# Routing attention and bilinear FFN on one core: row sums of the first batch element moved to VectorE, weight checks moved to ScalarE

## The chip, the cores and the metric

The kernel runs on one core of a Trainium2 chip. The time is the device time of one execution in microseconds (us), as the median of repeated runs. A profile of one execution shows what each engine did: TensorE (PE: matmuls, and PEld: its weight loads), VectorE (DVE), ScalarE (ACT), GpSimd (POOL) and SyncE (SP), whose queue issues most transfers. All five work through their own instructions in order and wait for each other by semaphores.

## What is computed

Attention with a mask by clusters, then a feed-forward block (FFN) with a product of two linear maps. There are 4 batch elements, 8 heads, 768 positions and 64 values per head; the FFN goes from 512 to 1536 and back, on 3072 tokens.

```python
q_assign = argmax(einsum('bhsd,hcd->bhsc', q_n, c_n))      # the nearest of 16 centroids
k_assign = argmax(einsum('bhsd,hcd->bhsc', k_n, c_n))
mask   = q_assign[:, :, :, None] == k_assign[:, :, None, :]
scores = where(mask, scale * q @ k^T, -1e9)
attn   = exp(scores - max) / (sum + 1e-9)
x      = (attn @ v) as (4*768, 512)
out    = ((x @ w_a) * (x @ w_b)) @ w_out
```

The weights come as float64, read as 64-bit integers. The kernel makes float32 of them itself.

## The kernel before

Two heads form a pair; there are 16 pairs, 4 to a batch element (`HP` = 4). A pair has 12 units: 2 halves of the query positions (`hf`), each with 6 tiles of 128 key positions (`j`). The main loop goes through groups of 2 units, so 6 groups to a pair and 24 (`BG`) to a batch element; `l` is the place of the group in its pair. In group g TensorE computes the scores of the two units of g, and weighs `v` with the probabilities of the group before. The FFN of a batch element, cut into pieces, is strewn over later groups.

```python
def score(us):          # TensorE: one-hot masks times masks plus q times k; ScalarE: exp
    ...
    add(ohTs, True); add(qkTs, False); exp()

def add_up(u):          # sums of the probabilities over the key tiles of a half
    p, hf, j = where(u)
    if j == 0 or j == NJ - 1 and p < HP:
        return
    ...
    for a in range(2):
        many = p >= HP and (a == 1 or j in (2, 4))
        eng = nc.gpsimd if many else nc.vector
        eng.tensor_tensor(out=acc[:, a, :], in0=..., in1=probs[u][:, a, :], op=ALU.add)

def denominators(p, hf):   # ones times sums, on TensorE; for p < HP the last tile is added here
    terms = [acc]
    if p < HP:
        terms.insert(0, probs[p * UPP + hf * NJ + NJ - 1])
    for n, t in enumerate(terms):
        for a in range(2):
            nc.tensor.matmul(out=ps[a * D:(a + 1) * D, 0:HB], lhsT=ones, rhs=t[:, a, :], ...)
    nc.scalar.activation(out=den, in_=ps[:, 0:HB], func=AF.Copy, accum_out=stat[:, n:n + 1])

def normalize(p, hf):   # transpose, reciprocal, transpose on VectorE, then x times it on GpSimd
    return [across, invert, back, apply]
```

Each part of the weights (36 of 128x512) is loaded into one of two `raw` buffers, turned into float32 by four VectorE operations and a sum on GpSimd, and set to zero where the source is too small (below `SMALLEST` in the upper 32 bits, read as a float):

```python
def round_w(i):
    flush_w()
    ...                                            # four VectorE operations on raw
    nc.scalar.activation(out=size, in_=halves(FP32)[:, :, 1], func=AF.Abs)
    nc.gpsimd.tensor_tensor(out=w, in0=w, in1=rest, op=ALU.add)
    flush.append((w, size))

def flush_w():                                     # w = w * (size >= SMALLEST), on VectorE
    ...
```

For the pairs of the first batch element (p < HP) q and k are transposed by TensorE. From pair 4 on (`by_blocks`), VectorE transposes them, finds the nearest centroids, makes the one-hot masks and transposes those; eight transfers on SyncE's queue then put them into `ohT`, which the scores of the pair's first group read:

```python
def one_hot():
    nc.gpsimd.tensor_tensor(out=oh[KT], ..., op=ALU.subtract)
    v.tensor_tensor(out=oh[QT], ..., op=ALU.is_equal)
def one_hot_across():
    v.transpose(out=ohT, in_=oh...)
    for a in range(2):
        for kq in range(4):
            nc.sync.dma_start(out=ohTs[p][...], in_=ohT[r:r + NC, :])
```

The main loop, in the order in which the instructions are queued:

```python
due = {3 * i + 1: [i] for i in range(8)}           # the group in which a part is rounded
for i in range(8, len(w_parts)):
    due.setdefault(23 + int((i - 8) / 1.5), []).append(i)
...
for g in range(NG + 3):
    p, l = divmod(g, GPP)
    if 0 < g < NG: score(now)
    check_inverses()
    if 0 < g <= NG:
        for u in before: add_up(u)
    flush_w()
    if 0 < g <= NG: weigh(before)
    if g < NG: ready[l]()                          # steps that prepare the next pair
    late = int(g > EARLY)                          # EARLY = BG + 1
    if g % 3 == late and 0 < g - late:
        denominators(*divmod(g // 3 - 1, 2))
    round_next()                                   # round_w(i), then load_w(i + 2)
    first, second = (4, 1) if g <= EARLY else (5, 3 if g < NG else 2)
    ...                                            # normalize the half that is due
    ...                                            # pieces of the FFN, as far as the credit goes
    round_next()
    while todo: todo.popleft()()                   # what ready and normalize left to do
    ...                                            # transposes and loads of coming pairs
```

Ahead of the loop the masks of pair 0 are made, and TensorE fills its gaps there with idle transposes (`keep_busy`).

Of the kernel before, what the change touches and what calls it, by code (L numbers as in the profile page):

```python
# [26 lines left out]
SIGN_EXP = 0xFF800000 - 2 ** 32  # L27

SMALLEST = 1.125 * 2.0 ** -15

P = 128
SCALE = 0.125
# [3 lines left out]
def kernel(  # L36
# [94 lines left out]
                          skip_runtime_bounds_check_because="a count of rows")  # L131
    with tc.If(redo > 0):
        with ExitStack() as slow:
            long_path(nc, tc, slow, c, q, k, v, out)


def short_path(nc, tc, ctx, c, cn, centroids_in, casts, n_far, q, k, v,
# [51 lines left out]
    def load(p):  # L189
        if p >= NPAIR:  # L190
            return
        b, hp = divmod(p, HP)
        if by_blocks(p):
            t = qkp.tile([P, 2, S // 32, 32], FP32, name="qk")
            for w, src in enumerate((q, k)):
                for n in range(4):
                    a, d = divmod(n, 2)
                    nc.sync.dma_start(
                        out=t[32 * n:32 * n + 32, w],
                        in_=src[b, 2 * hp + a, :, 32 * d:32 * d + 32].rearrange(  # L200
                            "(j t) d -> t j d", t=32))
            qks[p] = t
            return
        t = qkp.tile([P, 2, NJ, 2, D], FP32, name="qk")
        for w, src in enumerate((q, k)):
            for a in range(2):
                nc.sync.dma_start(
                    out=t[:, w, :, a, :],
                    in_=src[b, 2 * hp + a].rearrange("(p j) d -> p j d", j=NJ))
        qks[p] = t  # L210
# [30 lines left out]
            in_=v[b, 2 * hp:2 * hp + 2].rearrange("a (p j) d -> p a (j d)", j=NJ))  # L241

    first = load_first()
    centroids_in()
    order_first(*first, 0, nc.vector.tensor_copy)
    order_first(*first, 1, nc.scalar.copy)
# [14 lines left out]
        nc.sync.dma_start(out=raw, in_=w_parts[i][1])  # L261
        raws[i] = raw

    flush = []

    def round_w(i):
        flush_w()
        w = w_parts[i][0]
        wi = w.bitcast(INT32)
        raw = raws.pop(i)  # L270
        halves = lambda dt: raw.bitcast(dt).rearrange("p (n two) -> p n two", two=2)
        lo, hi = halves(UINT32)[:, :, 0], halves(INT32)[:, :, 1]


        nc.vector.tensor_scalar(out=wi, in0=hi, scalar1=3, scalar2=0x3FFFFFF8,
                                op0=ALU.logical_shift_left,
                                op1=ALU.bitwise_and)
        nc.vector.scalar_tensor_tensor(out=wi, in0=hi, scalar=SIGN_TOP, in1=wi,
                                       op0=ALU.bitwise_and, op1=ALU.bitwise_or)

        rest = wtp.tile([P, WN], FP32, name="rest")
        nc.vector.tensor_scalar(out=rest.bitcast(INT32), in0=wi,
                                scalar1=SIGN_EXP, scalar2=None,
                                op0=ALU.bitwise_and)
        nc.vector.scalar_tensor_tensor(out=rest, in0=lo, scalar=2.0 ** -52,
                                       in1=rest, op0=ALU.mult, op1=ALU.mult)

        size = sizep.tile([P, WN], FP32, name="size")
        nc.scalar.activation(out=size, in_=halves(FP32)[:, :, 1], func=AF.Abs)
        nc.gpsimd.tensor_tensor(out=w, in0=w, in1=rest, op=ALU.add)  # L290
        flush.append((w, size))

    def flush_w():

        while flush:
            w, size = flush.pop(0)
            nc.vector.scalar_tensor_tensor(out=w, in0=size, scalar=SMALLEST,
                                           in1=w, op0=ALU.is_ge, op1=ALU.mult)

    stat = zero.tile([P, 4 * NPAIR], FP32, name="stat")  # L300
    nfar = zero.tile([P, 1], FP32, name="nfar")
    nc.vector.memset(nfar, -FAR)

# [32 lines left out]
    def prep_transpose(p, i):  # L336
        if i == 0:
            qkTs[p] = qtp.tile([P, 2 * S], FP32, name="qkT")
        ps = ps_m.tile([P, 512], FP32, name="m")
        for n in range(4):  # L340
            w, j = divmod(4 * i + n, NJ)
            nc.tensor.transpose(  # L342
                out=ps[:, n * P:(n + 1) * P],
                in_=qks[p][:, w, j].rearrange("p a d -> p (a d)"),
                identity=ident)
        dst = qkTs[p][:, i * 512:(i + 1) * 512]
        if p == 0 and i != 1:
            nc.vector.tensor_copy(out=dst, in_=ps)
        else:
            nc.scalar.copy(out=dst, in_=ps)  # L350
# [146 lines left out]
    def prep_steps(p):  # L497
        if p >= NPAIR:
            return [lambda: None] * 6

        def both(*fs):
            return lambda: [f() for f in fs]

        if by_blocks(p):
            steps = prep_by_blocks(p)
            ready = [lambda s=s: todo.extend(s) for s in steps]
            ready[1] = both(lambda: prep_sim(p), lambda: load_v(p), ready[1])
            return ready

        return [  # L510
            both(lambda: prep_transpose(p, 0), lambda: prep_transpose(p, 1)),
            both(lambda: prep_sim(p), lambda: load_v(p)),
            lambda: todo.extend(prep_assign(prep_across(p))),
            lambda: None,
            lambda: prep_onehot(p, 1),
            lambda: None,
        ]
# [40 lines left out]

    def add_up(u):
        p, hf, j = where(u)  # L560
        if j == 0 or j == NJ - 1 and p < HP:
            return
        if j == 1:
            accs[p, hf] = accp.tile([P, 2, HB], FP32, name="acc")
        acc = accs[p, hf]
# [3 lines that stand above are left out]
            eng.tensor_tensor(  # L569
                out=acc[:, a, :],  # L570
                in0=probs[u - 1][:, a, :] if j == 1 else acc[:, a, :],
                in1=probs[u][:, a, :], op=ALU.add)
# [19 lines left out]

    def denominators(p, hf):


        ps = ps_m.tile([P, 512], FP32, name="m")
        acc = accs.pop((p, hf))
        terms = [acc]
        if p < HP:
            terms.insert(0, probs[p * UPP + hf * NJ + NJ - 1])  # L600
        for n, t in enumerate(terms):
            for a in range(2):
                nc.tensor.matmul(out=ps[a * D:(a + 1) * D, 0:HB], lhsT=ones,  # L603
                                 rhs=t[:, a, :], start=(n == 0),
                                 stop=(n == len(terms) - 1))
        den = acc[:, 0, :]
        n = 4 * p + 2 * hf
        nc.scalar.activation(out=den, in_=ps[:, 0:HB], func=AF.Copy,
                             accum_out=stat[:, n:n + 1])
        den_of[p, hf] = acc  # L610
# [367 lines left out]
    def ffn_ready(p, hf):  # L978
# [28 lines left out]
    PER_GROUP = [int(cols / n) + 1 for cols, n in (  # L1007
        (UP + DOWN * 7 / 8, BG + 5.8), ((UP + DOWN) * 7 / 8, BG + 0.8),
        ((UP + DOWN) * 7 / 8, BG + 0.5))]
    EARLY = BG + 1  # L1010
    credit = 0

# [1 line left out]
    for i in range(8, len(w_parts)):  # L1016
        due.setdefault(23 + int((i - 8) / 1.5), []).append(i)

    keep_busy(18)
    prep_transpose(0, 0)  # L1020
    centroids_across()
    prep_transpose(0, 1)
# [2 lines left out]
    for r, factor in ((slice(0, P // 2), 1.0), (slice(P // 2, P), FAR)):  # L1025
        nc.vector.tensor_scalar(out=rank_far[r], in0=rank[r], scalar1=factor,
                                scalar2=None, op0=ALU.mult)
    load(1)
    load_v(0)
    load_w(0)  # L1030
    load_w(1)
# [3 lines left out]

    across = prep_across(0)
    rest_of_first = score((0, 1))
    keep_busy(4)
    for kq in range(2):
        for step in prep_assign(across, kq):  # L1040
            step()
        prep_onehot_first(kq)
        if kq == 0:
            keep_busy(5)
            rest_of_first()
            keep_busy(7)
    for g in range(NG + 3):
        p, l = divmod(g, GPP)
        if l == 0:
            ready = prep_steps(p + 1)  # L1050
        now = (2 * g, 2 * g + 1)
        before = (2 * g - 2, 2 * g - 1)
        if 0 < g < NG:
            score(now)
        check_inverses()
        if 0 < g <= NG:
            for u in before:
                add_up(u)
        flush_w()
        if 0 < g <= NG:  # L1060
            weigh(before)
        if g < NG:
            ready[l]()
        late = int(g > EARLY)
        if g % 3 == late and 0 < g - late:
            denominators(*divmod(g // 3 - 1, 2))
        parts = due.get(g, [])

        def round_next():
            if parts:  # L1070
                i = parts.pop(0)
                round_w(i)
                load_w(i + 2)

        round_next()
        if g <= EARLY:
            first, second = 4, 1
        else:
            first, second = 5, 3 if g < NG else 2
        ph = {first: (p, 0), second: (p - 1, 1)}.get(l)  # L1080
        halved = ph in den_of
        if halved:
# [16 lines left out]
        if halved:  # L1099
            ffn_ready(*ph)  # L1100
        if l == 0 and p + 1 < NPAIR:
            if not by_blocks(p + 1):
                prep_transpose(p + 1, 2)
            load(p + 2)
        if l == 4 and p + 1 < NPAIR and not by_blocks(p + 1):
# [7 lines left out]

    some_ffn(6)
    check_inverses()
    fine = zero.tile([P, 4 * NPAIR], FP32, name="fine")
    nc.vector.tensor_scalar(out=fine, in0=stat, scalar1=LIMIT, scalar2=None,
                            op0=ALU.is_le)
    least = zero.tile([P, 1], FP32, name="least")
# [9 lines left out]
    some_ffn(len(ffn))  # L1129


def long_path(nc, tc, ctx, c, q, k, v, out):

    B, H, S, D = q.shape
    NC = 16
# [15 lines left out]
    ps_o = pool("l_ps_o", 1, PS)  # L1151
    ident, rank, cT = c["ident"], c["rank"], c["cT"]
    R = 2 * NC


    far = lone.tile([R, 2], FP32, name="far")
# [198 lines left out]
```

## Time and profile before

| what | value |
|---|---|
| time, median of 3 runs | 1052.72 us (1052.52 to 1053.35) |
| span of the profile | 1050.6 us |
| PE busy | 1036.5 us, 99% |
| DVE busy | 709.6 us, 68% |
| POOL busy | 355.7 us, 34% |
| ACT busy | 260.6 us, 25% |
| granted TensorE clock, mean | 0.999 |

The first part of the page gives the busy time of every engine. Matmuls overlap in the records, so the busy time of PE is not a sum of the single durations, and the mean of one matmul is longer than the distance to the next. The chain of waits follows the work that ended last back to its beginning: each piece has a start, a length, an engine and a line of the kernel. A timeline lists the instructions of a stretch in order of time, with the idle time ahead of one in brackets. Instruction names are given as output<-inputs.

### The profile page before, as it was taken

The numbers are of one execution on the slowest core, as the hardware profiler recorded it, in microseconds if no ns is written. First come the engines' busy times: TensorE is split into PE (matmuls) and PEld (weight loads), VectorE is DVE, ScalarE is ACT, GpSimd is POOL, SyncE is SP. The second block draws the span as 40 slices with busy tenths as digits, with TensorE's granted clock in tenths as the row PEclk, the third lists the DMA queues.
The fourth block names the chain that finished last, engine by engine and source line by source line (L and its number), as shares of the span: only waits on it lengthen the run. The fifth ranks groups of instructions, "written<-read, shape, count | busy, mean of one in ns | idle before, by whom it ended". The sixth has DMA issues, their size and how long they took to land.

```text
span 1050.6 us, 17937 instructions
## 1 busy us (share of the span) xinstructions
PE 1036.5 (99%) x7156; PEld 510.6 (49%) x7156; DVE 709.6 (68%) x1402; ACT 260.6 (25%) x501; POOL 355.7 (34%) x329
## 2 busy tenths in 40 slices
PE   8999999999999999999999999999999999999997
PEld 5444444444445554444444555444444565444576
DVE  5778878787857548676767746767665846776752
ACT  5666333333322221212222121122121200000000
POOL 1111244555542323443545422444344310212200
PEclk9999999999999999999999999999999999999999
DMA  5334243526230130303020030300000000000001
GB/s 167 89 75 109 69 122 88 126 81 143 64 50 16 33 53 18 44 4 46 4 46 1 25 66 20 51 1 20 1 4 1 12 31 22 1 1 1 2 32 34
DMA packets 120523, 46.49 MB, mean 44 GB/s; under 512 B 106608, under 2 KB 115824, under 8 KB 120432
## 3 DMA queue, kind: packets, MB, share of 16 engines
q1 hardware_dynamic: 120016, 44.85, 18.4%
q8 instruction: 58, 0.95, 0.4%
q10 hardware_dynamic: 416, 0.43, 0.1%
q14 instruction: 33, 0.27, 0.1%
HBM read 37.78 MB, written 6.29 MB: 42 GB/s over the span
## 4 chain that ended last, share of the span: by engine, by line
PE 92%; DVE 5%; issue 1%; POOL 1%; ACT 0%; DMA 0%; DVEq 0%; POOLq 0%
PE m L654 61%; PE s L539 14%; PE O L580 12%; PE m L603 2%; PE m L358 1%; DVE raw L730 1%; PE m L342 1%; POOL xT L635 1%; DVE raw L757 0%; DVE xT L730 0%; DVE raw L874 0%; DVE ha L784 0%; DVE acc L630 0%; DVE acc L569 0%; DVE acc L623 0%
## 5 line engine op out<-in xcount | busy, mean ns | idle before, releaser
L548 ACT ACTIVATE pt<-s 128x768 f32<-128x768 f32 x192 | 145.4, 808 | 303.3 <-PE s L539 250.3
L569 POOL TENSOR_TENSOR acc<-acc,pt 128x384 f32<-128x384 f32 x144 | 152.8, 1076 | 57.9 <-ACT pt L548 41.9
L789 POOL TENSOR_TENSOR h<-h,ha 128x384 f32<-128x384 f32 x72 | 73.0, 1021 | 230.9 <-DVE ha L784 230.9
L580 PE MATMUL O<-pt,v 128*64 128x384 f32 x768 | 145.0, 499 | 0.0
L539 PE MATMUL s<-qkT 64*128 64x384 f32 x768 | 139.6, 483 | 0.0
L654 PE MATMUL m<-xT,wa_sb 128*64 128x384 f32 x672 | 119.3, 487 | 1.7 <-POOL xT L635 0.9
L654 PE MATMUL m<-xT,wb_sb 128*64 128x384 f32 x672 | 119.1, 486 | 0.0
L784 DVE TENSOR_TENSOR ha<-ha,m 128x384 f32<-128x384 f32 x126 | 66.9, 546 | 70.7 <-PE m L654 69.6
L784 DVE TENSOR_TENSOR h<-h,m 128x384 f32<-128x384 f32 x126 | 67.2, 548 | 61.1 <-PE m L654 60.4
L569 DVE TENSOR_TENSOR acc<-acc,pt 128x384 f32<-128x384 f32 x96 | 73.7, 793 | 36.0 <-POOL acc L569 35.1
L580 PEld LDWEIGHTS O<-pt,v 128*64 128x64 f32 x768 | 46.6, 136 | 86.2 <-issue 86.1
L654 PE MATMUL m<-wo_sb,h 128*64 128x256 f32 x768 | 86.7, 379 | 0.0
L539 PEld LDWEIGHTS s<-qkT 64*128 64x128 f32 x768 | 70.5, 187 | 31.4 <-issue 0.2
L635 POOL TENSOR_TENSOR xT<-xT,acc 128x384 f32<-128x384 f32 x32 | 33.0, 1033 | 143.4 <-DVE acc L630 143.4
L654 PEld LDWEIGHTS m<-xT,wa_sb 128*64 128x64 f32 x672 | 49.2, 137 | 61.3 <-issue 50.6
L654 PEld LDWEIGHTS m<-xT,wb_sb 128*64 128x64 f32 x672 | 49.2, 137 | 59.3 <-issue 55.4
L654 PE MATMUL m<-raw 128*64 128x384 f32 x384 | 70.2, 486 | 1.1 <-DVE ha L784 1.1
L654 PEld LDWEIGHTS m<-wo_sb,h 128*64 128x64 f32 x768 | 57.3, 137 | 28.3 <-issue 3.9
L654 PE MATMUL m<-xT,h 128*64 128x256 f32 x576 | 64.8, 379 | 0.1
L654 PEld LDWEIGHTS m<-xT,h 128*64 128x64 f32 x576 | 43.0, 137 | 20.9 <-issue 2.9
L654 PE MATMUL m<-xT,size 128*64 128x384 f32 x288 | 52.6, 486 | 0.0
L539 PE MATMUL s<-ohT 64*128 64x384 bf16 x384 | 48.1, 328 | 0.5 <-DVE ohT L441 0.5
(160 smaller groups left out, 1267.8 us busy)
## 6 DMA issues: line engine op xcount, KB each, us to landing
raw<-in_moe_w_a_dram SPq DMA_DIRECT2D x12, 512.0 KB, 4.2
raw<-in_moe_w_b_dram SPq DMA_DIRECT2D x12, 512.0 KB, 3.6
raw<-in_moe_w_out_dram SPq DMA_DIRECT2D x12, 512.0 KB, 3.7
qk<-in_q_dram SPq DMA_DIRECT2D x48, 96.0 KB, 3.2
qk<-in_k_dram SPq DMA_DIRECT2D x48, 96.0 KB, 3.6
v<-in_v_dram SPq DMA_DIRECT2D x24, 192.0 KB, 3.8
out_dram<-rest SPq DMA_DIRECT2D x24, 128.0 KB, 1.7
v<-in_v_dram SPq DMA_DIRECT2D x4, 384.0 KB, 4.3
```

The source lines that it names most:

```text
L342: nc.tensor.transpose(out=ps[:, n * P:(n + 1) * P], in_=qks[p][:, w, j].rearrange("p a d -> p (a d)"), identity=ident)
L358: nc.tensor.matmul(out=ps[32 * kq:32 * kq + 32, 0:HB], lhsT=cTb[:, hp, :], rhs=qkTs[p][:, kq * HB:(kq + 1) * HB], start=True, stop=True)
L539: nc.tensor.matmul(out=s[:, a, 0:HB], lhsT=Ts[p][r, S + j * P:S + (j + 1) * P], rhs=Ts[p][r, hf * HB:(hf + 1) * HB], start=start, stop=not ...
L548: nc.scalar.activation(out=pt, in_=s[:, :, 0:HB], func=AF.Exp, scale=SCALE)
L569: eng.tensor_tensor(out=acc[:, a, :], in0=probs[u - 1][:, a, :] if j == 1 else acc[:, a, :], in1=probs[u][:, a, :], op=ALU.add)
L580: nc.tensor.matmul(out=O_of[0][a * D:(a + 1) * D, 0:HB], lhsT=vs[p][:, a, j, :], rhs=probs[u][:, a, :], start=(j == 0), stop=(j == NJ - 1))
L603: nc.tensor.matmul(out=ps[a * D:(a + 1) * D, 0:HB], lhsT=ones, rhs=t[:, a, :], start=(n == 0), stop=(n == len(terms) - 1))
L635: nc.gpsimd.tensor_tensor(out=x, in0=x, in1=den, op=ALU.mult)
L654: nc.tensor.matmul(out=ps[half], lhsT=lhsT[:, half], rhs=rhs, start=start, stop=stop)
L730: nc.vector.tensor_tensor(out=out, in0=l, in1=r, op=ALU.subtract)
L784: nc.vector.tensor_tensor(out=out, in0=in0, in1=ps, op=op)
L789: nc.gpsimd.tensor_tensor(out=to, in0=to, in1=box[name], op=ALU.mult)
```

## The change

It has five parts.

1. The last key tile of each half is now added on VectorE in the first batch element too, so the denominators need two matmuls there, not four. So that the sum is there in time, they are taken one group later (g % 3 == 1), as was done already in the later batch elements.
2. The halves of the first batch element are normalized one group later (places 5 and 2, not 4 and 1). The first pieces of the FFN become ready with the last pair's first half, so they too come a group later.
3. Subnormal weights are no longer set to zero in place. ScalarE takes Abs as before, and then Relu of (SMALLEST - size) * STEEP with a sum; if any such weight is there, the sum sends the kernel on its long path, which now does the flush. VectorE's flush is gone from the short path. Until the FFN has begun, the two ScalarE operations are queued at the top of the next group, and the load of the part after next goes with them.
4. Pair 1 is loaded at the very start, into a tile `h`, and its twelve transposes are moved from group 0 into gaps ahead of the loop, in place of idle ones. One of the three copies goes to VectorE.
5. In group 1 `weigh` comes ahead of `score`; twelve small matmuls are put ahead of the first idle transposes.

```diff
-        t = qkp.tile([P, 2, NJ, 2, D], FP32, name="qk")
+        own, name = (hp_, "h") if p == 1 else (qkp, "qk")
+        t = own.tile([P, 2, NJ, 2, D], FP32, name=name)
 ...
     first = load_first()
+    load(1)
     centroids_in()
 ...
-        size = sizep.tile([P, WN], FP32, name="size")
-        nc.scalar.activation(out=size, in_=halves(FP32)[:, :, 1], func=AF.Abs)
         nc.gpsimd.tensor_tensor(out=w, in0=w, in1=rest, op=ALU.add)
-        flush.append((w, size))
-    def flush_w(): ...
+        def check_size():
+            size = sizep.tile([P, WN], FP32, name="size")
+            n = 4 * NPAIR + i
+            nc.scalar.activation(out=size, in_=halves(FP32)[:, :, 1], func=AF.Abs)
+            nc.scalar.activation(out=size, in_=size, func=AF.Relu, scale=-STEEP,
+                                 bias=edge[:, 0:1], accum_out=stat[:, n:n + 1])
+            load_w(i + 2)
+        return check_size
 ...
-        if p == 0 and i != 1:
+        if p == 0 and i != 1 or p == 1 and i == 2:
             nc.vector.tensor_copy(out=dst, in_=ps)
 ...
-            both(lambda: prep_transpose(p, 0), lambda: prep_transpose(p, 1)),
+            lambda: p > 1 and (prep_transpose(p, 0), prep_transpose(p, 1)),
 ...
-        if j == 0 or j == NJ - 1 and p < HP:
+        if j == 0:
             return
 ...
-        terms = [acc]
-        if p < HP:
-            terms.insert(0, probs[p * UPP + hf * NJ + NJ - 1])
-        for n, t in enumerate(terms): ...
+        for a in range(2):
+            nc.tensor.matmul(out=ps[a * D:(a + 1) * D, 0:HB], lhsT=ones,
+                             rhs=acc[:, a, :], start=True, stop=True)
 ...
-    keep_busy(18)
+    for _ in range(12):
+        nc.tensor.matmul(out=idle[0:D, 0:D], lhsT=ones, rhs=ones, start=True, stop=True)
+    keep_busy(16)
 ...
-    load(1)
     load_v(0)
 ...
-    keep_busy(4)
+    prep_transpose(1, 0)
+    keep_busy(1)
     for kq in range(2):
         for step in prep_assign(across, kq):
             step()
+        if kq == 1:
+            prep_transpose(1, 1)
+            prep_transpose(1, 2)
         prep_onehot_first(kq)
         if kq == 0:
             keep_busy(5)
             rest_of_first()
-            keep_busy(7)
 ...
+        if g == 1:
+            weigh(before)
         if 0 < g < NG:
             score(now)
         check_inverses()
+        while sizes:
+            sizes.pop()()
         if 0 < g <= NG:
             for u in before:
                 add_up(u)
-        flush_w()
-        if 0 < g <= NG:
+        if 1 < g <= NG:
             weigh(before)
+        if g % 3 == 1 and g > 1:
+            denominators(*divmod(g // 3 - 1, 2))
         if g < NG:
             ready[l]()
-        late = int(g > EARLY)
-        if g % 3 == late and 0 < g - late:
-            denominators(*divmod(g // 3 - 1, 2))
 ...
-                i = parts.pop(0)
-                round_w(i)
-                load_w(i + 2)
+                check_size = round_w(parts.pop(0))
+                if ffn:
+                    check_size()
+                else:
+                    sizes.append(check_size)
 ...
-        if g <= EARLY:
-            first, second = 4, 1
-        else:
-            first, second = 5, 3 if g < NG else 2
+        first, second = 5, 3 if BG + 2 < g < NG else 2
```

Cut from the diff: the long path's flush of the weights, and the names of what it is handed. The long path isn't entered with the inputs used here.

More of the change, by code (lines that the diff above doesn't have):

```diff
@@ L29 @@
 SMALLEST = 1.125 * 2.0 ** -15
+STEEP = float(2 ** 100)
 P = 128
@@ L133 @@
         with ExitStack() as slow:
-            long_path(nc, tc, slow, c, q, k, v, out)
+            long_path(nc, tc, slow, c, q, k, v, moe_w_a, moe_w_b, moe_w_out, out)
 def short_path(nc, tc, ctx, c, cn, centroids_in, casts, n_far, q, k, v,
@@ L262, in load_w @@
         raws[i] = raw
-    flush = []
     def round_w(i):
-        flush_w()
         w = w_parts[i][0]
@@ L286, in round_w @@
                                        in1=rest, op0=ALU.mult, op1=ALU.mult)
-        size = sizep.tile([P, WN], FP32, name="size")
-        nc.scalar.activation(out=size, in_=halves(FP32)[:, :, 1], func=AF.Abs)
         nc.gpsimd.tensor_tensor(out=w, in0=w, in1=rest, op=ALU.add)
-        flush.append((w, size))
[L293 to L300, printed above, removed]
+        def check_size():
[6 more added lines that the diff above has]
+        return check_size
+    NSTAT = 4 * NPAIR + len(w_parts)
+    edge = zero.tile([P, 1], FP32, name="edge")
+    nc.vector.memset(edge, SMALLEST * STEEP)
+    stat = zero.tile([P, NSTAT], FP32, name="stat")
     nfar = zero.tile([P, 1], FP32, name="nfar")
@@ L597, in denominators @@
         acc = accs.pop((p, hf))
-        terms = [acc]
-        if p < HP:
-            terms.insert(0, probs[p * UPP + hf * NJ + NJ - 1])
[L601 to L605, printed above, removed]
+        for a in range(2):
+            nc.tensor.matmul(out=ps[a * D:(a + 1) * D, 0:HB], lhsT=ones,
+                             rhs=acc[:, a, :], start=True, stop=True)
         den = acc[:, 0, :]
@@ L1009, in short_path @@
         ((UP + DOWN) * 7 / 8, BG + 0.5))]
-    EARLY = BG + 1
     credit = 0
+    sizes = []
     due = {3 * i + 1: [i] for i in range(8)}
@@ L1017, in short_path @@
         due.setdefault(23 + int((i - 8) / 1.5), []).append(i)
-    keep_busy(18)
+    for _ in range(12):
+        nc.tensor.matmul(out=idle[0:D, 0:D], lhsT=ones, rhs=ones, start=True,
+                         stop=True)
+    keep_busy(16)
     prep_transpose(0, 0)
@@ L1058, in short_path @@
                 add_up(u)
-        flush_w()
-        if 0 < g <= NG:
+        if 1 < g <= NG:
             weigh(before)
+        if g % 3 == 1 and g > 1:
+            denominators(*divmod(g // 3 - 1, 2))
         if g < NG:
             ready[l]()
-        late = int(g > EARLY)
-        if g % 3 == late and 0 < g - late:
-            denominators(*divmod(g // 3 - 1, 2))
         parts = due.get(g, [])
@@ L1101, in short_path @@
         if l == 0 and p + 1 < NPAIR:
-            if not by_blocks(p + 1):
+            if p and not by_blocks(p + 1):
                 prep_transpose(p + 1, 2)
@@ L1115, in short_path @@
     check_inverses()
-    fine = zero.tile([P, 4 * NPAIR], FP32, name="fine")
+    fine = stat
     nc.vector.tensor_scalar(out=fine, in0=stat, scalar1=LIMIT, scalar2=None,
@@ L1129, in short_path, with long_path @@
     some_ffn(len(ffn))
-def long_path(nc, tc, ctx, c, q, k, v, out):
+def long_path(nc, tc, ctx, c, q, k, v, moe_w_a, moe_w_b, moe_w_out, out):
     B, H, S, D = q.shape
@@ L1153, in long_path @@
     R = 2 * NC
+    parts = [(sb[:, ch, n:n + DM], src[ch * P:(ch + 1) * P, n:n + DM])
+             for sb, src in ((c["wa_sb"], moe_w_a), (c["wb_sb"], moe_w_b))
+             for ch in range(NCH) for n in range(0, NF * P, DM)]
+    parts += [(c["wo_sb"][:, f, :], moe_w_out[f * P:(f + 1) * P, :])
+              for f in range(NF)]
+    for w, src in parts:
+        raw = lp.tile([P, DM], INT64, name="raw")
+        nc.sync.dma_start(out=raw, in_=src)
+        size = lp.tile([P, DM], FP32, name="size")
+        nc.scalar.activation(
+            out=size, in_=raw.bitcast(FP32).rearrange(
+                "p (n two) -> p n two", two=2)[:, :, 1], func=AF.Abs)
+        nc.vector.scalar_tensor_tensor(out=w, in0=size, scalar=SMALLEST, in1=w,
+                                       op0=ALU.is_ge, op1=ALU.mult)
     far = lone.tile([R, 2], FP32, name="far")
```

## The prediction

> **What bounds the kernel now.** I read the busy times first, then the chain of waits, whole and for the first 130 us, and then timelines around the places that the change touches. The page gives the chain by engine and line:
>
> ```profile
> PE 92%; DVE 5%; issue 1%; POOL 1%; ACT 0%; DMA 0%; DVEq 0%; POOLq 0%
> ```
>
> TensorE carries nearly all of it. A matmul taken off that chain is time gained if nothing else comes late, and a new wait of TensorE is time lost. From the chain of the first 130 us (start, length, engine and line):
>
> ```profile
> 18.37 0.66 PE m L342 x4
> 19.03 1.72 PE s L539 x12
> 20.75 1.44 PE O L580 x8
> 22.19 0.78 PE m L358 x8
> 22.97 1.72 PE s L539 x12
> ...
> 29.78 1.65 PE m L603 x7
> ...
> 42.77 1.44 PE m L603 x8
> ```
>
> From 19.03 on TensorE's pieces touch each other. A group of two units is 1.72 us of scores (L539) and 1.44 us of weighing (L580), 3.16 in all. L603 is the denominators: eight instructions, since the trace has two for each of the four fp32 matmuls.
>
> The place that decides, I think, is where the second batch element begins: group 24, whose scores read `ohT`. Timelines of PE, SP and DVE:
>
> ```profile
> 112.83 2.10 PE L654 MATMUL m<-xT,wa_sb 128*64 128x384 f32 x12
> 115.82 0.87 PE L654 MATMUL m<-xT,wa_sb 128*64 128x384 f32 x4 [0.88 <-POOL xT L635]
> ...
> 121.78 0.50 PE L539 MATMUL s<-ohT 64*128 64x384 bf16 x4
> ```
>
> ```profile
> 110.07 0.35 SPq L261 DMA_DIRECT2D raw<-in_moe_w_b_dram  x1
> 113.15 5.03 SPq L480 DMA_DIRECT2D ohT<-oh  x8
> ```
>
> ```profile
> 112.55 0.58 DVE L476 STREAM_TRANSPOSE oh<-oh 128x384 bf16<-128x384 bf16 x1 [2.08 <-POOL oh L470]
> ```
>
> VectorE transposes the masks at 112.55, SyncE needs until 118.2 to issue the eight transfers, each landing 1.8 us after its issue (median for this tile), so `ohT` is complete at about 119.5. TensorE doesn't notice: three pieces of FFN (L654) stand before the scores of group 24 and fill 112.8 to 121.8.
>
> **What the Trainium skill says.** "SBUF — State Buffer", section "Who interferes with whom": a VectorE instruction with two SBUF inputs and a GpSimd instruction that reads SBUF exclude each other. The trace agrees:
>
> ```profile
> 106.74 1.01 DVE L569 TENSOR_TENSOR acc<-pt 128x384 f32<-128x384 f32 x2
> ...
> 114.39 2.73 DVE L569 TENSOR_TENSOR acc<-acc,pt 128x384 f32<-128x384 f32 x4
> ```
>
> The pair ran alone, 0.47 us from one addition to the next; the four ran beside GpSimd's L635 (114.63 to 115.77) and took 0.7 more than twice as long. "TensorE: Matmul & The Clock Gate", part 1: after an idle window of about 3.4 us the array falls to half its clock, and needs as long to recover. The start agrees: the first 18 idle transposes took 4.10 us, 0.23 each, and 8 of the same shape at 17.15 took 1.04, 0.13 each. "Perfetto Trace Analysis", "Identifying the Most-Contended Engine", warns that matmul busy time is no measure of headroom. The trace shows why: the mean L654 matmul of 384 columns is listed with 487 ns, and 16 of them take 2.58 us on the chain, 0.16 each. So I count from the chain, not from the 99%.
>
> **The change, part by part.**
>
> *Denominators.* The four removed instructions take 0.65 us (29.61 to 30.25 in the timeline, and half of the clean 1.29 us of the same line at 93.30). Before, some also waited for the last addition. The pieces of the first five half-pairs on the chain are 1.65, 1.44, 1.65, 1.44, 1.65, together 7.83 (at 29.78, 42.77, 55.55, 68.55 and 81.32). After, 5 x 0.65 = 3.25, and a group later the sum is ready. Gain **4.6 us**. The other three half-pairs fall into the stretch that I work out below.
>
> *Pair 1's transposes.* Now TensorE ends the transposes at 19.03, scores until 20.75, weighs until 22.19. After, the transposes lie at about 12.7 and 15.6 to 16.7, in gaps that held idle transposes; the last one-hot transposes still end at 17.3 and their copies at 18.3 to 18.4. Weighing comes first and fills 17.3 to 18.75; the scores of group 1 follow to 20.5. Gain 22.19 - 20.5 = **1.7 us**. The early load shares the start with k (landed at 5.44, copied at 5.47), whose copies have some 0.6 us to spare, and the earlier warm-up may save a few tenths; I set both to zero.
>
> *Weight checks.* 36 flushes of 0.69 us leave VectorE; ScalarE gets 36 times some 0.9 us (Abs with as many elements takes 0.69, its read of an accumulator 0.19 at L608). ScalarE is 25% busy, so this costs nothing on the path, apart from tenths where groups are short. In groups 24 to 41 VectorE is relieved by some 19 us, but TensorE isn't waiting for it there: nothing on the chain, **0**.
>
> *More additions.* 16 additions of 0.47 us move to VectorE, 4 to a pair.
>
> *The FFN a group later.* Here the gain is given back. I follow both engines from the start of group 18 (90.07 before), as time since then.
>
> Before: masks transposed at 22.5 to 23.0, `ohT` landed at 29.4, group 24 at 31.7 with three FFN pieces done.
>
> After, VectorE: it ends the normalization of pair 2's first half, now a group later, at 3.4; four additions beside GpSimd (2.7) to 6.1; two transposes (1.9) to 8.0; two additions, rounding (2.25) and sims to 11.8; four additions to 14.2; two of the four assign steps (1.1) to 15.3; normalization (1.4) to 16.7; four additions beside GpSimd to 19.4, where before there were two; two assign steps to 20.5; additions and rounding to 23.7; GpSimd's weight sum and half mask (1.5 and 0.85 us in the trace of before) to 26.3; transposes to 26.9; eight issues of 0.63 to 32.0; landed at about **33.2**.
>
> TensorE: group 19 has denominators and L358 and, with a wait for the transposes, ends at 8.4; groups 20 and 21 take 3.2 each, to 14.8; group 22 waits for the late sum of its denominators to about 20.0; group 23 ends at 23.3. No FFN stands in group 23 now, so TensorE waits from **23.3 to about 33**. Then scores and weighing, at first at half clock, to 37 or 38.
>
> Behind it a second wait: the load of part 9 is queued after the eight transfers, is issued at 32.0 and lands 3.65 later (3.64 for the one at 110.07), at 35.7; VectorE must round it (2.25) before it gets to the normalization of pair 3's first half (1.4), GpSimd's product follows to 40.5. The first FFN piece needs it for its last quarter. So its end is at 41.2 and three pieces are done at 46.3. By the same count of work the kernel before stands at 31.7 + 3.16 = 34.9. Loss **11.4 us**. If VectorE instead keeps the pace that it has now (`ohT` at 28.5), the same steps give a loss of 7. I take **10**.
>
> *The last half-pair's denominators.* Group 24 took 132.54 - 121.78 = 10.76 us, of which 3.16 and two pieces of 2.58 leave 2.44 for denominators with their wait; after, 0.65. Gain **1.8**.
>
> Sum: -4.6 - 1.7 - 1.8 + 10 = +1.9, so 1052.7 + 1.9 = **1054.6 us**.
>
> **Rivals.** *A: the pure sum of what was taken off TensorE*, 8 half-pairs and the transposes, some 11 us, giving 1042. For it speaks that TensorE is the bound everywhere; against it that `ohT` landed only 2.3 us before it was needed, behind 9 us of FFN that are now gone. *B: my stall, but short*, because VectorE, rid of the flush, makes the masks sooner: with a loss of 5 it is 1049.6. Against it: in pair 3 VectorE loses two flushes (1.4 us) and gains four additions (1.9). *C: more stalls than I see*: the probabilities have four buffers, and an exp now waits for VectorE's additions two groups back; with VectorE at some 22 of 24 us in each early pair a wait of 0.5 us in each of 20 groups would make 1065. Against it: by my count VectorE falls back two groups behind at most and catches up while it waits for the next assign.
>
> **Range and chances.** The gains are sure to a microsecond; the loss lies between 5 and 15. So 1049 to 1060. Two per cent are 21 us; neither A nor C gets there.
>
> **What would show it.** In the changed kernel's profile: L603's fp32 instructions with `pt` gone; scores of group 1 ending near 20.5; a gap of TensorE of some 5 to 10 us before the first scores of pair 4, ended by the transfers into `ohT`, then a shorter one ended by L635's product. If the first gap is under 3 us, my order of VectorE is wrong and rival A or B holds; if many gaps lie before group 18, C does.

## The result and the profile after

The changed kernel took 1059.16 us (median of 6 runs, 1058.7 to 1059.67) against 1052.62 us of the kernel before on the same chip: a ratio of 1.0062 with a 95% interval of 1.0049 to 1.0075. It is slower, by some 6.5 us.

The chain of waits by engine and line, and the slices of the page (each a fortieth of the span, busy tenths of TensorE and the clock that it was granted):

```profile
PE 87%; DVE 7%; issue 2%; DMA 1%; SPq 1%; POOL 1%; ACT 0%; DVEq 0%; POOLq 0%
```

```profile
PE   9999699999999999999999999999999999999997
...
PEclk9999899999999999999999999999999999999999
```

TensorE's share of the chain fell from 92% to 87%, and one slice stands out: the fifth, from 105.7 to 132.2 us, where TensorE was busy six tenths and the clock fell. What was to be gained can be seen ahead of it. The chain between 17 and 33 us:

```profile
17.11 1.44 PE O L587 x8
18.55 1.72 PE s L546 x12
20.27 0.78 PE m L365 x8
21.06 1.82 PE s L546 x12
...
31.12 0.65 PE m L605 x4
```

Weighing now precedes the scores of group 1, the transposes of pair 1 are gone from this stretch, and the scores of group 2 start at 21.06, not at 22.97. The denominators (L605) take 0.65 us, not 1.65. When group 18 begins, the changed kernel is 4.9 us ahead (at 85.14 us, where the kernel before is at 90.00).

Then the timeline of TensorE (start, length; in brackets the idle time before, and what ended it):

```profile
106.24 1.51 PE L587 MATMUL O<-pt,v 128*64 128x384 f32 x8
114.15 0.50 PE L546 MATMUL s<-ohT 64*128 64x384 bf16 x1 [6.40 <-DMA ohT<-oh]
116.69 0.82 PE L546 MATMUL s<-ohT 64*128 64x384 bf16 x3 [2.04 <-DMA ohT<-oh]
116.98 3.08 PE L546 MATMUL s<-qkT 64*128 64x384 f32 x8
119.99 2.08 PE L587 MATMUL O<-pt,v 128*64 128x384 f32 x8
121.91 2.10 PE L655 MATMUL m<-xT,wa_sb 128*64 128x384 f32 x12
125.06 0.87 PE L655 MATMUL m<-xT,wa_sb 128*64 128x384 f32 x4 [1.05 <-POOL xT L636]
```

TensorE has nothing to do until the masks of pair 4 land in `ohT`: 6.40 and 2.04 us. The next eight matmuls take 3.08 us where the same eight take 1.45 elsewhere. A view by stretches (busy time and count of PE, PEld, DVE, ACT and POOL, granted clock, share of DMA, GB/s) shows why:

```profile
105.00:115.00 10.00, 3.25 (x19) 1.01 (x15) 7.72 (x16) 3.17 (x7) 2.35 (x2) 0.80 0.02 6
115.00:120.00 5.00, 3.31 (x12) 2.24 (x13) 0.20 (x2) 0.81 (x1) 1.26 (x1) 0.50 0.41 118
```

After the pause the clock was granted at half, as the Trainium skill says in "TensorE: Matmul & The Clock Gate", part 1, of idle windows of about 3.4 us: 0.50 from 115 to 120 us. It cost some 1.6 us on those eight and 0.6 on the weighing. The third wait, 1.05 us, is for GpSimd's product, and VectorE's and SyncE's timelines show what stands behind it:

```profile
110.45 0.58 DVE L483 STREAM_TRANSPOSE oh<-oh 128x384 bf16<-128x384 bf16 x1 [2.08 <-POOL oh L477]
...
119.92 0.43 DVE L278 TENSOR_SCALAR wb_sb<-raw 128x512 int32<-128x512 int32 x1 [4.80 <-DMA raw<-in_moe_w_b_dram]
```

```profile
111.06 5.03 SPq L487 DMA_DIRECT2D ohT<-oh  x8
116.20 8.74 SPq L267 DMA_DIRECT2D raw<-in_moe_w_b_dram  x2
```

The load of part 9 went out behind the eight transfers, and VectorE stood still for it with the normalization of pair 3 queued behind.

### The profile page after: what moved, and what is told of

Read it like the earlier page. It is cut to its first block, busy times and chain, and to the rows that moved or that the text cites. A ratio compares the mean times of both kernels' runs of the same rounds, so it can differ in the third digit from the quotient of the medians.

```text
span 1057.5 us, 17946 instructions
## 1 busy us (share of the span) xinstructions
PE 1032.4 (98%) x7136; PEld 511.2 (48%) x7136; DVE 712.4 (67%) x1384; ACT 288.6 (27%) x572; POOL 357.6 (34%) x329
## 4 chain that ended last, share of the span: by engine, by line
PE 87%; DVE 7%; issue 2%; DMA 1%; SPq 1%; POOL 1%; ACT 0%; DVEq 0%; POOLq 0%
PE m L655 59%; PE s L546 13%; PE O L587 11%; PE m L605 2%; PE m L365 1%; DVE acc L576 1%; DMA raw<-in_moe_w_b_dram 1%; DMA raw<-in_moe_w_a_dram 0%; PE m L349 0%; DVE raw L875 0%; SPq L201 0%; SPq L487 0%; DVE raw L758 0%; DVE acc L624 0%; DVE qkT L467 0%
## 5 line engine op out<-in xcount | busy, mean ns | idle before, releaser
L576 DVE TENSOR_TENSOR acc<-acc,pt 128x384 f32<-128x384 f32 x112 | 85.3, 795 | 31.2 <-POOL acc L576 31.2
```

The costliest lines, as they stand in the source:

```text
L576: eng.tensor_tensor(out=acc[:, a, :], in0=probs[u - 1][:, a, :] if j == 1 else acc[:, a, :], in1=probs[u][:, a, :], op=ALU.add)
```

## The experiments

Three theories were to be told apart. Theory 1: the loss comes from the FFN beginning one group later, so that nothing stands in front of pair 4's first scores while its masks are still on their way. Theory 2: VectorE's extra additions make the masks late. Theory 3: ScalarE's second pass over the weights holds things up. All times of one run are set against the kernel before on the same chip (1051.6 to 1052.0 us there).

### The delay of the FFN alone, in the kernel before

```diff
-        if g <= EARLY:
-            first, second = 4, 1
-        else:
-            first, second = 5, 3 if g < NG else 2
+        first, second = 5, 3 if BG + 2 < g < NG else 2
```

> The kernel before, with the halves of the first batch element normalized at places 5 and 2, so that the FFN begins one group later; sums, denominators and the VectorE flush stay as before. Theory 1 (the loss comes from FFN work no longer standing in front of the first scores of pair 4, while the masks of that pair are still on their way): a gap of TensorE of 5 to 7 us before those scores, ended by the transfers into ohT, and 1058 to 1063 us. Theory 2 (VectorE's extra additions make the masks late) and theory 3 (ScalarE's second pass over the weights holds it up): neither is in this kernel, so 1052 to 1054 us.

Measured: 1068.58 us, ratio 1.016 (1.0143 to 1.0177), more than any theory had said (the profiled execution took 1070.02 us). TensorE's timeline has the gap in the same place:

```profile
120.09 0.33 PE L539 MATMUL s<-ohT 64*128 64x384 bf16 x1 [3.27 <-DMA ohT<-oh]
122.62 0.82 PE L539 MATMUL s<-ohT 64*128 64x384 bf16 x3 [2.20 <-DMA ohT<-oh]
```

The gap of 5.5 us comes with the late FFN alone, without any of the new additions or checks. The rest I had not foreseen: groups 9 and 15 each lose 2.1 us, where their denominators, still at the old place, now wait for VectorE's sum (pauses of 1.0 and 0.4 us in each group); and a wait of 2.84 us follows at 172.9.

### Pair 3 as before, in the changed kernel

Its last tile is added by TensorE again, and its denominators and normalization come at the old places.

```diff
-        if j == 0:
+        if j == 0 or j == NJ - 1 and p == HP - 1:
...
+        if p == HP - 1:
+            terms.insert(0, probs[p * UPP + hf * NJ + NJ - 1])
...
+        if g in (BG - 3, BG):
+            denominators(*divmod(g // 3 - 1, 2))
...
+        if BG - 3 < g < BG + 2:
+            first, second = 4, 1 if g > BG else second
```

> The changed kernel, with pair 3 alone treated as before: its last key tile is added by TensorE again, its denominators and its normalization come where they came before, so the FFN begins in group 23. Theory 1: the gaps of 6.4 and 2.0 us at pair 4's first scores vanish, with them the half clock behind them; 1047 to 1050 us, faster than the kernel before. Theory 2: pair 3 has four additions fewer, so the masks come about 2 us sooner and 1056 to 1058 us. Theory 3: 1058 to 1060 us.

Measured: 1049.10 us, ratio 0.9973 (0.9963 to 0.9982): by the ratios some 9 us better than the changed kernel, and faster than the kernel before. The timeline:

```profile
102.19 0.86 PE L609 MATMUL m<-acc,ones 128*64 128x384 f32 x2 [1.38 <-DVE acc L576]
...
119.42 0.50 PE L546 MATMUL s<-ohT 64*128 64x384 bf16 x4
...
125.33 1.22 PE L609 MATMUL m<-acc,ones 128*64 128x384 f32 x3 [2.04 <-DVE acc L576]
```

The scores at 119.42 have no wait at all, though the masks here are transposed 24.4 us after the start of group 18, hardly sooner than in the changed kernel (25.3). That is the sharpest cut between theories 1 and 2: late masks cost nothing behind 9 us of FFN. What is left are denominators that wait for VectorE, 1.38 and 2.04 us. The profiled execution took 1051.49 us, the longest of ten: behind the 2.04 us the clock was granted at half (0.50 from 127 to 129 us), and fourteen matmuls took 3.92 us that take 2.56 in the kernel before. Whether the shorter executions had this too is not shown.

### No second pass on ScalarE

```diff
-            nc.scalar.activation(out=size, in_=size, func=AF.Relu, scale=-STEEP,
-                                 bias=edge[:, 0:1], accum_out=stat[:, n:n + 1])
```

The weights are not checked at all in this kernel.

> The changed kernel without the Relu pass on ScalarE, so that weights are not checked at all; Abs and the place of the loads stay. Theories 1 and 2: within 0.5 us of the changed kernel's 1059.2. Theory 3: 1053 to 1056 us.

Measured: 1058.10 us, ratio 1.0063 (1.0046 to 1.008), the ratio of the changed kernel (1.0062). The gaps are the same to 0.01 us (6.40 and 2.03). Theory 3 falls, for the place that the change gave these passes.

### The prologue alone, in the kernel before

The diff is that of the change: the early `load(1)` into `h`, `prep_transpose(1, ...)` in the gaps, the twelve small matmuls, `weigh` ahead of `score` in group 1.

> The kernel before with only the prologue of the change: pair 1 loaded at the start, its transposes in gaps ahead of the loop, the small warm-up matmuls, weighing ahead of scoring in group 1. All theories: 1.5 to 2.0 us faster than before, 1050.6 to 1051.1 us, group 2's first scores near 21.0 and not 22.9.

Measured: 1050.82 us, ratio 0.9989 (0.9981 to 0.9998), 0.8 us by the medians; the profiled spans differ by 2.0 us (1048.5 and 1050.6), and from group 2 to the end its trace is 1.9 us ahead, never more or less. The gain is real; its size by the clock of the whole program is not settled better than 0.2 to 2 us.

### The masks sooner

```diff
-                    assign[:2], assign[2:], [one_hot, one_hot_across], []]
+                    assign, [one_hot, one_hot_across], [], []]
```

> The changed kernel, with the steps that make pair 4's masks drawn together: all four assign steps in group 20, the one-hot steps in group 21, ahead of the rounding of part 7 and its sum on GpSimd. The FFN still begins in group 24. Theory 1 (TensorE waits for the masks, with nothing in front of them): VectorE's transpose of the masks comes about 5 us sooner than at 110.45, the two gaps of together 8.4 us shrink to 3 to 5 us, the load of part 9 moves up with them; 1053 to 1056 us. If the gap is made by anything but this chain, 1058 to 1060 us.

Measured: 1055.59 us, ratio 1.0031 (1.002 to 1.0041).

```profile
110.31 0.33 PE L546 MATMUL s<-ohT 64*128 64x384 bf16 x1 [0.20 <-ACT size L297]
112.85 0.50 PE L546 MATMUL s<-ohT 64*128 64x384 bf16 x3 [2.20 <-DMA ohT<-oh]
...
121.95 1.26 PE L655 MATMUL m<-xT,wa_sb 128*64 128x384 f32 x4 [3.94 <-POOL xT L636]
```

The masks were transposed at 106.61, 20.9 us after the start of group 18, 4.4 sooner than in the changed kernel. The load of part 9 moved up by as much, the gap fell from 8.4 to 2.4 us, and the eight matmuls behind it took 1.61 us, not 3.08. Much of that came back as other waits: 3.94 us for GpSimd's product, 1.05 before, and 1.75 and 0.62 us in group 22, where the changed kernel has one of 0.57. So the chain from masks over transfers to scores is confirmed, and so is a second wait behind it. But the load is no longer what holds the product up: VectorE waits only 0.59 us for it, and has two parts to round before it gets to the normalization.

### Two queues for the transfers

```diff
-                    nc.sync.dma_start(
+                    eng = nc.scalar if p == HP and kq % 2 else nc.sync
+                    eng.dma_start(
```

> The changed kernel, with four of pair 4's eight transfers into ohT issued by ScalarE and four by SyncE. Theory 1: the last transfer that the first scores need is issued 1.9 us sooner, so the gaps shrink from 8.4 to about 6.5 us and the load behind them is issued 2.5 us sooner; 1056.5 to 1057.5 us. If the issue isn't a part of the chain: 1058.5 to 1060 us.

Measured: 1058.66 us, ratio 1.0065 (1.0048 to 1.0081): not faster by the runs. In the trace the pauses before the scores are 7.25 us together in place of 8.44, and the wait in the first FFN piece is 2.02 in place of 1.05. The timelines of TensorE's weight loads, of its matmuls and of ScalarE:

```profile
114.47 0.10 PEld L547 LDWEIGHTS <-ohT 64*128 64x128 bf16 x2 [1.20 <-DMA ohT<-oh]
```

```profile
114.47 0.50 PE L547 MATMUL s<-ohT 64*128 64x384 bf16 x2 [7.05 <-ACT pt L556]
115.17 0.51 PE L547 MATMUL s<-ohT 64*128 64x384 bf16 x2 [0.20 <-ACT pt L556]
```

```profile
110.72 2.79 ACTq L488 DMA_DIRECT2D ohT<-oh  x4
113.61 1.51 ACT L556 ACTIVATE pt<-s 128x768 f32<-128x768 f32 x2 [8.68 <-DVE wa_sb L281]
```

The last weight load that waits for a transfer comes 29.7 us after the start of group 18, where the changed kernel has it at 31.5: the 1.9 us that I expected from the issue are there. But ScalarE's four issues wait for the masks, transposed at 110.11, and stand in its queue ahead of the exps of group 23, which began at 105.78 in the changed kernel and here begin at 113.61. The scores wait for these exps too, so that 1.2 of the 1.9 us are left. The pass over part 7 comes behind the exps (115.00 to 115.66), and the load of part 9, which needs that part's buffer, was issued at 115.69, hardly sooner than the 116.20 of the changed kernel. So GpSimd's product ended its wait 39.8 us after the start of group 18, as in the changed kernel (39.9), and the rest was lost there.

### Checks and loads right behind the rounding

```diff
-                if ffn:
-                    check_size()
-                else:
-                    sizes.append(check_size)
+                check_size()
```

> The changed kernel, with the two ScalarE passes over a part and the load of the part after next queued right behind its rounding, as the load was before, and not at the top of the next group. Theory 1: the gaps of 8.4 us stay; the load of part 9 no longer stands behind the eight transfers, VectorE's waits for it (4.8 us and 4.5 us) go, and with them the wait of 1.05 us in the first FFN piece; 1 to 2 us better than the changed kernel, 1057 to 1058 us. If the late loads made the loss: 1052 to 1054 us.

Measured: 1058.79 us, ratio 1.0063 (1.0046 to 1.008). The expectation missed half of it. At the critical place it did what was expected: the gap stays (6.43 and 2.04), VectorE's waits for the loads and the 1.05 us in the first FFN piece are gone, and from group 17 on it loses 3 us less than the changed kernel. But most of that had been lost before: at group 17 it is 2.2 us ahead of the kernel before, not 4.9. ScalarE's timeline shows where:

```profile
33.03 0.89 ACT L430 ACTIVATE ohT<-m,nfar 128x768 bf16<-128x768 bf16 x1
33.81 0.67 ACT L297 ACTIVATE size<-raw 128x512 f32<-128x512 f32 x1
34.51 0.72 ACT L298 ACTIVATE size<-size,edge 128x512 f32<-128x512 f32 x1
...
35.23 0.78 ACT L433 COPY ohT<-m 128x768 bf16<-128x768 bf16 x1
35.91 1.51 ACT L555 ACTIVATE pt<-s 128x768 f32<-128x768 f32 x2
```

The two passes stand between two mask copies, ahead of the exps, and the scores of groups 6, 12 and 18 each wait twice, 0.36 to 0.41 us. An engine that is busy 27% of the span can delay the path where its work is queued ahead of what the path needs: theory 3 was right about the engine, and the change had already avoided the case.

### Second halves normalized later still

```diff
-        first, second = 5, 3 if BG + 2 < g < NG else 2
+        first, second = 5, 3 if (g < BG - GPP or BG + 2 < g) and g < NG else 2
```

> The changed kernel, with the second halves of pairs 0 and 1 normalized at place 3, not 2. In the trace of the changed kernel ScalarE's check of the reciprocals, queued at the top of group 9, waits 1.8 us for VectorE, which is still at the masks of the next pair, and holds up the copy out of PSUM and the exps behind it; groups 10 and 16 lose about 1.0 us each that way. If so: 2 us better than the changed kernel, 1057 to 1057.5 us, the gaps before weighing at 53.7 and 78.5 gone. If the order of VectorE doesn't matter: 1059.

In the changed kernel ScalarE's timeline reads:

```profile
52.98 0.21 ACT L644 ACTIVATE inv<-inv 128x12 f32<-128x12 f32 x1 [1.79 <-DVE acc L631]
...
53.19 0.46 ACT L597 COPY xT<-O 128x384 f32<-128x384 f32 x1
54.76 1.75 ACT L555 ACTIVATE pt<-s 128x768 f32<-128x768 f32 x2 [1.11 <-DVE acc L576]
```

Measured: 1058.27 us, ratio 1.0059 (1.0042 to 1.0075), no difference by the runs. The waits in groups 10 and 16 are gone, and at group 18 the kernel is 6.6 us ahead in place of 4.9. But 1.5 us of the 1.7 are given back by group 20: counted from the start of group 18, VectorE ends the transposes of pair 4 at 8.6 us in place of 7.1, and the products with the centroids wait for them.

### Both together: the new sums for five halves, the FFN at its old place

The last three halves of the first batch element are treated as before, pair 2's second among them so that VectorE isn't late in pair 3; checks and loads follow the rounding at once from group 22 on.

```diff
+    OLD = 2 * HP - 3
...
-        if j == 0:
+        if j == 0 or j == NJ - 1 and OLD <= 2 * p + hf < 2 * HP:
...
+        if g % 3 == 0 and OLD <= g // 3 - 1 < 2 * HP:
+            denominators(*divmod(g // 3 - 1, 2))
...
+        if 3 * OLD + 3 <= g < BG + 2:
+            first, second = 4, 1
...
-                if ffn:
+                if ffn or g >= BG - 2:
                     check_size()
```

> The changed kernel, but the last three halves of the first batch element (pair 2's second, pair 3's both) have their last tile added by TensorE, and their denominators and normalization where they came before, so that the FFN begins in group 23; from group 22 on the weight checks and loads are queued right behind the rounding. The new sums stay for five halves, and so does the new prologue. Theory 1: at group 18 it is 4.9 us ahead of the kernel before, as the changed kernel is, and nothing is lost after that: 1047 to 1048 us, a ratio of 0.995 to 0.996, no gap before pair 4's first scores. If VectorE's additions in the early pairs make the masks late even so: 1049 to 1052.

> The same, with the second halves of pairs 0 and 1 normalized at place 3 rather than 2, which by group 18 gave another 1.7 us. If VectorE catches up by pair 3: 1045.5 to 1046.5 us. If it is given back there, as in the run that had this place alone: 1047 to 1048 us.

Measured: 1045.47 us, ratio 0.9935 (0.9921 to 0.9949), and 1044.82 us, ratio 0.9928 (0.9914 to 0.9941). Both beat both kernels, and by the intervals they are the same. The second one's timeline at the place of the loss:

```profile
110.87 0.87 PE L660 MATMUL m<-xT,wa_sb 128*64 128x384 f32 x4 [0.82 <-POOL xT L641]
111.57 2.75 PE L660 MATMUL m<-xT,wb_sb 128*64 128x384 f32 x16
...
116.83 0.50 PE L546 MATMUL s<-ohT 64*128 64x384 bf16 x4
```

They came out 2 us better than I expected, since they also gain after group 18: 5.1 us ahead there in the first, 7.6 at the end. Some 1.15 us come in group 24, where the denominators take 1.3 us and the kernel before needs 2.4 with its wait for the sum of pair 3. The rest, some 1.5 us, comes in groups 31 and 37. There the products with the centroids (L358 before) wait for VectorE's transposes, which in the kernel before end 3.6 and 4.2 us after the start of the group, and in the first combined kernel 0.1 us before it. VectorE's flush is gone, and that fits. But the changed order also puts the denominators (0.65 us) ahead of these products, where they hide a part of such a wait, and no run takes the two apart. The later normalization gains its 1.4 us by group 18 and gives them back in group 18, as denominators that wait for VectorE (0.81 and 0.41 us).

## Why the prediction was right

The time of 1059.16 us lies in the range, near its upper end, and 4.6 us above the point. The mechanism was the one predicted, step by step; the sizes were off by these terms. A rise of 1.9 us was forecast and 6.5 us measured: the point was the small remainder of a loss of 10 us and gains of 8.1, and no term but the prologue's came out better than I had it. The range held both signs, so that the right sign of the sum owes something to luck; what was foreseen is the place, the cause and the size of the loss behind group 18.

| step, from the start of group 18 where times are given | predicted | measured |
|---|---|---|
| gain of the prologue | 1.7 us | 1.9 us |
| gain of the first five denominators | 4.6 us | 3.0 us |
| masks landed in `ohT` | 33.2 | 32.1 |
| TensorE waits for them | 23.3 to 33, then half clock | 22.5 to 31.5 with one matmul between, then half clock |
| product of pair 3's first half ends its wait | 40.5 | 39.9 |
| three FFN pieces done | 46.3 | 45.9 |
| loss of that stretch | 11.4 worked out, 10 taken | 10.9 |
| gain of the last denominators | 1.8 us | 1.1 us, with the products beside them (L365) 0.6 slower |
| FFN after that | 0 | a loss of about 2.0 us, what is left of the 6.9 us between the two profiles |

- **The denominators.** Each costs 0.65 us, as predicted. Groups 10 and 16 of the changed kernel lost about 1.0 us each, which takes away the gain of the first halves of pairs 1 and 2; the whole term was 1.6 us too large. I had said that VectorE catches up while it waits for the next assign step. It does, but at place 2 the normalization comes behind that step, and ScalarE, whose check of the reciprocals is queued ahead of a copy and two exps, waits with it. Moving the normalization took these waits away, so this cause is shown.
- **The loss.** The order of VectorE that I wrote down was right within 1.1 us at the masks. My discount from 11.4 to 10, for a VectorE that might keep its old pace, was unfounded: counted from the start of group 18, the masks come 2.8 us later than before (25.3 against 22.5 us), where the delay of the FFN alone leaves them at 22.6. With pair 3 as before they come at 24.4, and with the second half of pair 2 as before too, in the first combined kernel, at 22.7. So VectorE's new work, from pair 2 on, makes them late; I did not try the additions apart from the later normalization in the changed kernel. By the clock of the program the masks come 2.1 us sooner than before (110.45 against 112.55), but TensorE asks for them 4.9 us sooner, and without the FFN in front. So theory 2 holds for a part of the gap's length (8.4 us, and 5.5 with the late FFN alone), and theory 1 for there being a gap.
- **The FFN after that.** I had put it at zero. Waits of 0.86 us at 165.5 and 1.50 us at 341.8 are new. Each of the seven kernels measured whose FFN begins in group 24 has waits of their kind at 0.3 to 2.8 and 1.5 us, and none of the five whose FFN begins in group 23 has them. Why a group of delay leads to just these was not tried.
- **Rivals.** A fell with the gap. B's short stall didn't come: the flush that VectorE was rid of is outweighed by the additions. C's many waits were two of 1.0 us, in groups 10 and 16, and one of 0.57 us in group 22, not one in every group.
- **The weight checks** cost nothing, as predicted, but only at the place that the change gave them. That VectorE's relief in the FFN is worth nothing is less sure: see groups 31 and 37 of the combined kernels.

## What to carry to other kernels

Before moving work to a later turn of a loop, ask what it stands in front of: 9 us of FFN were there as it were by chance, and hid a chain of GpSimd, VectorE and eight transfers that nobody had to look at. Write down the queue of every engine around such a joint, in order, with the durations of the trace; that found the loss of that stretch to 5%, where a sum of what leaves the busiest engine had the wrong sign. When a change gains in one stretch and loses at a joint, keep it in the stretch and undo it at the joint: that gave 0.993 of the time before, where the whole change gave 1.006.

## What the runs showed that was not expected

- ScalarE, busy 27% of the span, held up TensorE in three ways: by a check of 0.2 us that waits for VectorE, queued ahead of a copy (1.0 us a time); by 1.4 us of passes queued ahead of exps (two waits of about 0.4 us in each of three groups); and, in the run with two queues, by four issues of transfers that wait for the masks, queued ahead of exps (these began some 8 us later).
- Transfers of 12 KB took SyncE 0.63 us each to issue (eight in 5.03 us) where a load of 512 KB took 0.33 us in the median. In three of the kernels whose FFN begins in group 23, the eight took 5.78 to 6.22 us. Issuing them from two queues let the last one needed land 1.9 us sooner, as the issue times promised, and held up the exps on the second queue.
- The length of a pause alone did not tell whether the half clock followed. After pauses of 6.40 and 2.04 us, parted by one matmul, TensorE was granted half its clock from 115 to 120 us; after 3.27 and 2.20 us in the kernel with the late FFN alone, it was granted 0.50 from 122.5 to 125 us and the eight matmuls took 2.96 us. With the masks sooner, a pause of 2.20 us left the clock at 1.00, and one of 3.94 us brought it to 0.50 (sixteen matmuls in 4.10 us, not 2.75). But with pair 3 as before a single pause of 2.04 us was followed by 0.50, though it is shorter than the 3.4 us named above.
